# The sequence transform's A11 B11 for two blocks at once, in seven quarter products

## The chip, the core and the metric

The kernel runs on one core of one Trainium2 chip. The core has TensorE (matmuls from SBUF into PSUM), VectorE and ScalarE (elementwise work on SBUF and PSUM), GpSimd (here it only issues DMAs and a few memsets) and SyncE (it only issues DMAs). Each engine carries out its own instructions in the order in which the program gives them; semaphores tie the engines together. The metric is the device time of one execution in microseconds, the median of several runs. 0.2% is about what a measurement of this kernel can tell from no change.

## The reference

With S = 2048 rows, D = 512 columns and F = 1376 hidden units, all in f32:

```python
a = x @ dft_hid_re.T;  b = x @ dft_hid_im.T
y = dft_seq_re @ a - dft_seq_im @ b            # FNet mixing, real part
h = silu(x @ w1) * (x @ w3);  z = h @ w2       # SwiGLU
g = sigmoid((x * gate_w).sum(-1))
out = g * y + (1 - g) * z
```

The DFT matrices are inputs like any other.

## The kernel before, in words

**Precision.** Each f32 operand is split into a high part (rounded to the fp32r type by ScalarE, `high`, line 110) and a low part (source minus high, by VectorE, `low`, line 113). A product is then three matmuls: high x high, high x low, low x high (`mm3`, line 124 issues each). Nearly all the work of ScalarE and VectorE is in making these parts and the sums below. Two such parts of a 128x1024 operand are one `zo` buffer (`parts`), of which there are two in the first stage and four later; whole 128x1024 f32 operands lie in the `F4` buffers (`wide`). Both are handed out and given back in order, by lists that the program keeps while it is built.

**Seven products for eight.** Each big product is cut into 2x2 blocks and made by the Winograd form of Strassen's method: seven block products instead of eight, with sums of blocks ahead (T1 to T4 on the moving side, S1 to S4 on the stationary one) and sums of products behind. In the code a product has a name P1 to P7 and a form: P1 takes B11, P5 T1, P6 T2, P3 B22, P7 T3, P2 B21, P4 T4. P1 = A11 B11 is a part of all four results.

**Stage one, gate/up.** 22 steps; step n is one chunk of 128 hidden units against one half of the sequence, made by `gate_up(n)`. A step is 42 matmuls in seven products into PSUM banks X, Y and Z. What matters here is the order: the products that `gate_up` issues are X(4), Z(5), the first product of step n+3, X(3), Z(2), the second of step n+3, and X(6). Between them VectorE has, in this order: what `early` holds for the step (the low part of one operand of the second half, `xo`, and its sum, line 206), four sums for the weights of the next step (lines 245 to 248), `u4 += x` (line 368), the low part of these weights (`wb`), `u2 += z` (373), `u2 *= s1` (374), the low part of another weight (`wa`), and `g1 *= u4` (390), and last what `at_end` holds for the step. The X bank is read by line 368 and then accumulated into by X(6). The lists `early`, `ahead`, `second`, `mid`, `at_end` are dictionaries from a step to functions, filled by `do`. In the same stage the weights' wb parts go to DRAM and come back for the second half, the results h go to DRAM (line 323), and from step 9 on the operands of the next stages (w2 and the transformed inputs A1) are prepared, at the steps in `W2_AT` and `A1_AT`.

**Stage two, the sequence transform ("F").** Four blocks of 512 output columns. The stationary side is A = the transformed inputs (A1, A2, from x), the moving side are the DFT matrices (`cc`), whose blocks are loaded, summed, split and used once. `STEPS` is one list of steps (block, quarter of the contraction, product, form); an F block has 28 steps of 12 matmuls, four for each product. (b, n) below is step n of block b, counting blocks from 0. `advance(m)`, called in step m behind its matmuls, asks for the loads of step m+8 where F4 has a free buffer, makes the sum of step m+4 and the split of step m+3. A zo buffer comes free when TensorE has finished the step that used it. SyncE issues the loads in that order too, and waits in its queue for a buffer's last reader. When P1 is done, ScalarE copies its two banks into the banks of P2 (line 945), so that both go on accumulating. Results are multiplied by the gate and put to DRAM by `spill` (lines 815 to 818). Beside that, "late" pieces (one of w2, four of the hidden DFT `dd`) are loaded, summed, split and put to DRAM, by `late_load` and the functions after it, at given (b, n).

**Stages three and four** ("H", two blocks: h times w2; "Y", two blocks: the hidden DFT) use the same list of steps.

Of the kernel before, what the change touches and what calls it, by code (L numbers as in the profile page):

```python
# [7 lines left out]
F32 = mybir.dt.float32  # L8
# [4 lines left out]
P = 128  # L13
# [12 lines left out]
LOOK = 3  # L26
K = 9
TAIL = 256
W2_AT = (9, 11, 13, 15)
A1_AT = (12, 14, 16, 17, 18, 19, 20)  # L30


# [1 line left out]
def fnet_swiglu_gate_kernel(  # L34
# [103 lines left out]
    wbsp = dram.tile([NC, P, 2, 4, 256], F32, tag="wbsp", name="wbsp")  # L138
    zsp = dram.tile([4 * NTB * P, 1024], F32, tag="zsp", name="zsp")

    hsp = dram.tile([2, 4, (NP2 + 1) // 2, P, 1024], F32, tag="hsp", name="hsp")
    hlsp = dram.tile([2, P, 1024], F32, tag="hlsp", name="hlsp")

# [380 lines left out]
    for n, k in ((7, "B12"), (7, "B11"), (8, "B21"), (9, "B22")):  # L524
        do(early, n, lambda k=k: free(ST[1, k]))

    W2R = {}

    def load_w2(p):
# [67 lines left out]
    for k in range(LOOK + 2):  # L597
# [22 lines left out]
    STEPS = [(blk, q, k, form) for blk, nq in enumerate(NQ) for k, form in ORDER[blk]  # L620
             for q in range(nq)]
    START = [sum(NQ[:blk]) * len(CHAIN) for blk in range(NB + 1)]

    NEED = [(("B11", 0, 0), ("B12", 1, 1), ("B22", 2, 1), ("B21", 5 - (b == 0), 0))
            for b in range(NB - 1)]
# [10 lines left out]
    LOADS = sorted((START[blk] + n * nq - e * (blk > 0 or n != 1) + q, blk, k, q)  # L636
                   for blk, nq in enumerate(NQ) for q in range(nq) for k, n, e in NEED[blk])

    def z_rows(tb, k):
        return zsp[(tb * 4 + k) * P : (tb * 4 + k + 1) * P, :]  # L640

    def block(blk, k, q):
        if KIND[blk] == "F":
            return cc[blk, ("B11", "B12", "B22", "B21").index(k), q]
        if KIND[blk] == "H":
            return hsp[blk - NTB, ("B11", "B12", "B21", "B22").index(k), q]
        return z_rows(2 * (blk - NTB - 2) + (k in ("B12", "B22")), 2 * (k in ("B21", "B22")) + q)

    def cols(blk, q, form):

        return 512 if KIND[blk] == "H" and q == NQ[blk] - 1 else 1024

    def done(m, j):
        blk, q, k, form = STEPS[m]
        b = DONE[j].get(form)
        if b:
            free(RAW.pop((blk, b, q)))

    def sum_c(m):


        if not 0 <= m < len(STEPS):
            return
        blk, q, k, form = STEPS[m]
        b = {"T1": "B11", "T2": "B22", "T4": "B21"}.get(form)
        if b:
            n = cols(blk, q, b)
            t = RAW[blk, PLACE[form], q][:, :n]
            nc.vector.tensor_add(t, t, RAW[blk, b, q][:, :n])  # L669
        elif form == "T3":  # L670
            n = cols(blk, q, form)
            t = RAW[blk, "B11", q][:, :n]
            nc.vector.tensor_sub(t, RAW[blk, "B12", q][:, :n], t)  # L673
        done(m, 0)

    def split_c(m, parts_of=(0, 1)):
        if not 0 <= m < len(STEPS):
            return
        blk, q, k, form = STEPS[m]
        src = RAW[blk, PLACE.get(form, form), q]  # L680
# [33 lines left out]
    F4[:0] = [(f4_b, f"f4_{k}") for k in range(5 + LOOK, 13)]  # L714
    ZO[:0] = [(zo_b, f"zo_{k}") for k in range(2, 4)]
    def load_a2(p):

# [86 lines left out]
    XB, ZB, YB = ((4, 5), (6, 7)), (0, 2), (3, 1)  # L804
    U = {}

    def spill(blk, k, t, ps=None):


# [34 lines left out]
    def load_gate(blk):  # L844
        v = gsp if KIND[blk] == "F" else ngsp
        tbs = [blk] if KIND[blk] == "F" else [2 * (blk - NTB), 2 * (blk - NTB) + 1]
        GT[blk] = []
        for tb in tbs:
            t = ut.tile([P, 512], F32, tag="gate", name=f"gate{blk}_{tb}", bufs=2)
            nc.sync.dma_start(t, v[tb // 2, :, tb % 2 * 512 : (tb % 2 + 1) * 512])  # L850
            GT[blk].append(t)

    def load_nb(blk, k):
        tb = 2 * (blk - NTB - 2) + k // 2
# [17 lines left out]

    def step(m):
        blk, q, k, form = STEPS[m]
        kind = KIND[blk]
        if k == "P6" and kind != "Y" and q == 2 * (blk == 0):
            load_gate(blk)
        seeded = blk < NB - 1
# [111 lines left out]

            put(2, result)
        elif k == "P2" and seeded:
            put(1, lambda: spill(blk, 0, res("s1"), ps))
        elif k == "P2":
            plus("s1")
            spill(blk, 0, U["s1"])
        else:
            spill(blk, 1, res("c21"), ps)

    todo = {}  # L1000
    WL, HL = {}, {}
# [53 lines left out]
        free(*(HL.pop((blk, t)) for t in range(3)))  # L1055

    def at(blk, n, f, *a):
        todo.setdefault(START[blk] + n, []).append((f, a))

    at(1, 1, load_score, 1)  # L1060
    for p in range(NG):
# [7 lines left out]
    for g, n in enumerate((5, 3)):  # L1069
        for i in range(4):  # L1070
            at(g, n + i, gates, g, i)
    late = [(w2, w2sp, p) for p in range(len(W2_AT), NP2)] + [(dd, dsp, p) for p in range(KD)]
    for i, (src, sp, p) in enumerate(late):
        blk, b = 1 + i // 3, i % 3
        n = (10, 17, 24)[b]
        at(blk, n - (6, 5, 6)[b], late_load, i, src[p], ("u3", "s1", "u2")[b])
        at(blk, n, late_sums, i)
        at(blk, n + 1, late_split1, i)
        at(blk, n + 2, late_split2, i)
# [101 lines left out]
```

## Time and profile before

| | us |
|---|---|
| median of 3 runs | 674.63 (674.20 to 674.96) |
| the profiled execution | 674.75 |
| its span, first to last instruction | 673.0 |
| TensorE busy | 667.3 (99%) |
| VectorE busy | 577.2 (86%) |
| ScalarE busy | 370.0 (55%) |
| moved by DMA | 171 MB, mean 254 GB/s |

A row of the profile has the line, the engine, the operation, the names of output and inputs, their shapes and a count; then the busy time and the mean of one; then the idle time ahead of it and who ended that. Rows of the timeline begin with start and duration in us. In names, x2 and the like is a count of like instructions in one row; PE is TensorE, PEld its weight loads, DVE VectorE, ACT ScalarE, POOL GpSimd and SPq the DMA queue of SyncE. A matmul's duration is a latency and overlaps that of the next one.

### The profile page before, as it was taken

How to read it: one execution, taken by the hardware profiler on the slowest of the kernel's cores; microseconds unless marked ns; L12 is line 12 of the kernel's file. 1: busy time of each engine (PE TensorE's matmuls, PEld its weight loads, DVE VectorE, ACT ScalarE, POOL GpSimd, SP SyncE). 2: the span in 40 equal slices, each digit the busy share in tenths (PEclk: the TensorE clock that was granted, in tenths of full speed). 3: DMA queues.
4: the chain of work that ended last, by engine and by line, in shares of the span. 5: the costliest groups of instructions: out<-in, count | busy, mean ns of one | idle time of the engine just before them, and what ended most of it. 6: DMA issues, size and time to landing. Idle time of an engine off the chain costs nothing.

```text
span 673.0 us, 8613 instructions
## 1 busy us (share of the span) xinstructions
PE 667.3 (99%) x3101; PEld 580.5 (86%) x3101; DVE 577.2 (86%) x685; ACT 370.0 (55%) x472; POOL 61.9 (9%) x114
## 2 busy tenths in 40 slices
PE   8999999999999999999999999999999999999997
PEld 6888888888888888888888888888888888888886
DVE  6979877787679999988999799868798698798896
ACT  6765556656546874465454655444446446446452
POOL 0011112121110000101120101000000010010000
PEclk9999999999999999999999999999999999999999
DMA  7685655599986956644697277719888795784942
GB/s 296 213 304 222 236 217 205 205 349 372 424 364 240 361 196 236 250 155 152 239 373 298 80 254 276 281 34 349 308 323 238 238 378 166 312 300 173 339 126 94
DMA packets 46010, 171.23 MB, mean 254 GB/s; under 512 B 5520, under 2 KB 5904, under 8 KB 42256
## 3 DMA queue, kind: packets, MB, share of 16 engines
q1 hardware_dynamic: 33376, 118.90, 49.5%
q0 software_dynamic: 12160, 51.13, 19.3%
q10 hardware_dynamic: 432, 0.66, 0.3%
q8 instruction: 24, 0.39, 0.2%
q14 instruction: 18, 0.15, 0.1%
HBM read 115.34 MB, written 55.32 MB: 254 GB/s over the span
## 4 chain that ended last, share of the span: by engine, by line
PE 99%; DMA 1%; ACT 0%; SPq 0%; issue 0%
PE P L124 68%; PE X L124 16%; PE Z L124 8%; PE Y L124 4%; PE C L124 2%; DMA xs_B<-xt 1%; PE V L124 0%; PE P4left L124 0%; ACT xo L110 0%; ACT zc L834 0%; SPq L223 0%
## 5 line engine op out<-in xcount | busy, mean ns | idle before, releaser
L124 PE MATMUL P<-zo,a 128*128 128x512 f32 x1344 | 290.3, 379 | 0.0
L110 ACT ACTIVATE zo<-B 128x1024 fp32r<-128x1024 f32 (+1 forms) x182 | 185.5, 1022 | 182.8 <-PE P L124 99.6
L124 PEld LDWEIGHTS P<-zo,a 128*128 128x128 f32 x1344 | 253.9, 189 | 36.2
L113 DVE TENSOR_TENSOR zo<-B,zo 128x1024 fp32r<-128x1024 f32 (+1 forms) x182 | 213.5, 1178 | 33.1 <-ACT zo L110 32.4
L669 DVE TENSOR_TENSOR B<-B,B 128x1024 f32<-128x1024 f32 (+1 forms) x78 | 91.6, 1175 | 0.1
L124 PE MATMUL P<-zo,H 128*128 128x512 f32 x420 | 91.3, 379 | 0.0
L124 PEld LDWEIGHTS P<-zo,H 128*128 128x128 f32 x420 | 79.2, 189 | 11.8 <-issue 0.7
L124 PE MATMUL X<-xo,wb 128*128 128x512 f32 x378 | 88.9, 380 | 0.0
L124 PEld LDWEIGHTS X<-xo,wb 128*128 128x128 f32 x378 | 71.2, 189 | 10.6 <-DMA wb<-wbsp 0.3
L124 PE MATMUL P<-zo,Y 128*128 128x512 f32 (+1 forms) x336 | 71.6, 375 | 0.0
L124 PEld LDWEIGHTS P<-zo,Y 128*128 128x128 f32 x336 | 62.7, 189 | 8.7
L323 POOL DMA_DIRECT2D hsp<-h x40 | 21.9, 547 | 112.4 <-DVE h L374 67.9
L385 ACT ACTIVATE h<-X 128x512 f32<-128x512 f32 x21 | 12.5, 596 | 35.1 <-PE X L124 35.1
L124 PE MATMUL Z<-xo,wa 128*128 128x512 f32 x126 | 30.6, 379 | 0.0
L124 PE MATMUL Z<-xo,wb 128*128 128x512 f32 x126 | 30.6, 379 | 0.0
L673 DVE TENSOR_TENSOR B<-B,B 128x1024 f32<-128x1024 f32 (+1 forms) x26 | 30.6, 1177 | 0.0
L124 PE MATMUL X<-xo,wa 128*128 128x512 f32 x126 | 30.5, 379 | 0.0
L124 PE MATMUL Y<-xo,wa 128*128 128x512 f32 x126 | 30.5, 379 | 0.0
L124 PEld LDWEIGHTS X<-xo,wa 128*128 128x128 f32 x126 | 23.8, 189 | 3.4
L124 PEld LDWEIGHTS Y<-xo,wa 128*128 128x128 f32 x126 | 23.8, 189 | 3.4
L124 PEld LDWEIGHTS Z<-xo,wb 128*128 128x128 f32 x126 | 23.8, 189 | 3.4
L124 PEld LDWEIGHTS Z<-xo,wa 128*128 128x128 f32 x126 | 23.8, 189 | 3.4
(158 smaller groups left out, 548.6 us busy)
## 6 DMA issues: line engine op xcount, KB each, us to landing
B<-cc SPq DMA_DIRECT2D x64, 512.0 KB, 6.3
hsp<-h POOLq DMA_DIRECT2D x40, 256.0 KB, 4.3
wbsp<-wb POOLq DMA_DIRECT2D x8, 1024.0 KB, 4.2
wb<-wbsp SPq DMA_DIRECT2D x8, 1024.0 KB, 8.3
B<-hsp SPq DMA_DIRECT2D x16, 512.0 KB, 8.2
B<-zsp SPq DMA_DIRECT2D x16, 512.0 KB, 7.1
ws<-w SPq DMA_DIRECT2D x11, 512.0 KB, 5.4
H<-w2sp SPq DMA_DIRECT2D x5, 1024.0 KB, 8.5
```

The lines of the kernel that those rows point to most:

```text
L110: nc.scalar.activation(hi, src, AF.Copy)
L113: nc.vector.tensor_sub(lo, src, hi.bitcast(F32))
L124: nc.tensor.matmul(ps.rearrange("p (n a) -> p n a", a=2), u, turns(v)[:, some], **kw)
L323: nc.gpsimd.dma_start(hsp[g, b + k, j // 2, :, j % 2 * 512 : (j % 2 + 1) * 512], h)
L385: nc.scalar.activation(g1, x, AF.Silu)
L669: nc.vector.tensor_add(t, t, RAW[blk, b, q][:, :n])
L673: nc.vector.tensor_sub(t, RAW[blk, "B12", q][:, :n], t)
```

## The change

A11 B11 of block 2 and A11 B11 of block 3 have the same stationary side. The change takes B11 of both blocks as one matrix, cuts A11 (256 rows by 1024) and that matrix into 2x2 quarters, and makes the four quarters of the product by the same seven-product form one level down: m1 to m7, each of two steps of six matmuls.

- The eight P1 steps of blocks 2 and 3 go (`todo_p1`); what hung on them moves to the step after (`NEW`).
- The 14 new steps stand among steps (1,22) to (1,27) and (2,4) to (2,9), after the step that `AMONG` names: m1a; m1b and m6a; m6b; m7a; m7b; m4a and m4b; m2a; m2b; m5a; m5b; m3a; m3b.
- The sums of the moving quarters (T1 to T4 of the second level, each in two halves h) are made in gate/up: `load_quarters(h)` loads four 512 KB quarters into the two zo buffers at the end of step 2 (h = 0) and 5 (h = 1), `sum_quarter` makes one sum by VectorE and GpSimd puts it to DRAM (`tsp`), at the ends of steps 3, 4, 4, 5 and 6, 7, 8, 9. In the F stage they are loaded again like any other operand.
- The sums of the stationary side (`load_s`, `sums_s`, `high_s`, `low_s`) are made in block 1.
- `step_quarter` makes a step: m1 into bank 5, which ScalarE copies to bank 4; m6, m7 and m4 accumulate into bank 5, with ScalarE putting aside the state after m6 and after m7; m2 goes to bank 4; m5 to bank 7, to which VectorE adds the two states set aside (into banks 6 and 7); m3 into bank 6. Banks 4, 5 are then P1 of block 2, and 6, 7 of block 3. `seeds` makes the copies for P2.
- Of the late pieces, those at (1,17), (1,24) and (2,17) go to (3,10), (3,17) and (5,4). The first w2 piece of gate/up goes from step 9 to 10. F4 gets one buffer more; the gates one less, and for H a different one; block 1's P2 and P4 results leave from another buffer (u3).

```diff
-W2_AT = (9, 11, 13, 15)
+W2_AT = (10, 11, 13, 15)
...
+    def load_quarter(h, b, t):
+        BQ[h, b] = t
+        nc.sync.dma_start(t, cc[2 + (b[2] == "2"), 0, 2 * (b[1] == "2") + h])
+
+    def load_quarters(h):
+        for b in ("b11", "b12"), ("b21", "b22"):
+            t = BQ[h, b] = parts(f"q{h}{b[0]}")
+            v = t.bitcast(F32).rearrange("p h a n -> p h (a n)")
+            for i in range(2):
+                load_quarter(h, b[i], v[:, i])
+
+    def sum_quarter(h, i):
+        to, u, v = (("b11", "b12", "b11"), ("b22", "b22", "b11"),
+                    ("b12", "b22", "b12"), ("b21", "b21", "b22"))[i - 1]
+        nc.vector.tensor_sub(BQ[h, to], BQ[h, u], BQ[h, v])
+        nc.gpsimd.dma_start(tsp[i - 1, h], BQ[h, to])
+
+    for h, at_n in enumerate(((2, 3, 4, 4, 5), (5, 6, 7, 8, 9))):
+        do(at_end, at_n[0], load_quarters, h)
+        for n, i in zip(at_n[1:], (1, 3, 2, 4)):
+            do(at_end, n, sum_quarter, h, i)
+        do(at_end, at_n[4], lambda h=h: free(BQ[h, ("b11", "b12")], BQ[h, ("b21", "b22")]))
...
+    AMONG = {(1, 22): ("m1a",), (1, 23): ("m1b", "m6a"), (1, 24): ("m6b",), (1, 25): ("m7a",), (1, 26): ("m7b",),
+             (1, 27): ("m4a", "m4b"), (2, 4): ("m2a",), (2, 5): ("m2b",), (2, 6): ("m5a",),
+             (2, 7): ("m5b",), (2, 8): ("m3a",), (2, 9): ("m3b",)}
...
+            if blk in (2, 3) and k == "P1":
+                todo_p1.append(START[blk] + n)
+                continue
...
+    def step_quarter(m):
+        _, h, k, _ = STEPS[m]
+        zt = ZT.pop(m)
+        z = zt.rearrange("p h a n -> p h (a n)")
+        to = {"m2": 4, "m5": 7, "m3": 6}.get(k, 5)
+        own = k in ("m1", "m5")
+        if own and h == 0:
+            MB[to] = bank(to, f"quarter{to}")
+        for i in range(2):
+            b = slice(i * 512, (i + 1) * 512)
+            mm3(MB[to], *quarter(k, h, i), z[:, 0, b], z[:, 1, b], own and h == i == 0, h == i == 1,
+                not own)
+        free(zt)
+        advance(m)
+        if h == 0:
+            return
+        if k == "m1":
+            MB[4] = bank(4, "quarter4")
+            nc.scalar.activation(MB[4], MB[5], AF.Copy)
+        elif k == "m6":
+            MB["u"] = ut.tile([P, 2, 512], F32, tag="u2", name="uu")
+            nc.scalar.activation(MB["u"][:, 0], MB[5], AF.Copy)
+        elif k == "m7":
+            nc.scalar.activation(MB["u"][:, 1], MB[5], AF.Copy)
+            free(*SF[0])
+        elif k == "m2":
+            seeds(2, MB[4], MB[5])
+        elif k == "m5":
+            MB[6] = bank(6, "quarter6")
+            nc.vector.tensor_add(MB[6], MB[7], MB["u"][:, 0])
+            nc.vector.tensor_add(MB[7], MB[7], MB["u"][:, 1])
...
+    LATES = (1, 10, "u3"), (2, 10, "u3"), (3, 10, "u3"), (3, 17, "s1"), (NTB + 1, 4, "s1")
```

More of the change, by code (lines that the diff above doesn't have):

```diff
@@ L649, in cols @@
     def cols(blk, q, form):
-        return 512 if KIND[blk] == "H" and q == NQ[blk] - 1 else 1024
+        return 512 if form[0] != "m" and KIND[blk] == "H" and q == NQ[blk] - 1 else 1024
     def done(m, j):
         blk, q, k, form = STEPS[m]
+        if k[0] == "m":
+            return free(RAW.pop((4, k, q))) if j and form != "B11" else None
         b = DONE[j].get(form)
@@ new lines, in high_s, with low_s, quarter @@
+    def high_s(i):
+        SF[i] = [take(F4, [P, 1024], F32R, f"s{i}{k}") for k in "hl"[: 2 - i]]
+        if i:
+            SF[i].append(ut.tile([P, 1024], F32R, tag="s1", name="s1l"))
+        high(SF[i][0], flat(SR[i]))
+    def low_s(i):
+        low(*SF[i], flat(SR[i]))
+    def quarter(k, h, i):
+        kk = 2 * h + i
+        if len(QUARTERS[k]) == 3:
+            _, r, half = QUARTERS[k]
+            w = A1[4 * half + kk][:, :, 1, r * P : (r + 1) * P]
+            return w[:, 0], w[:, 1]
+        t, at = {"m6": (0, 0), "m7": (0, P), "m3": (1, 0), "m5": (1, P)}[k]
+        return [v.rearrange("p (k n) -> p k n", k=4)[:, kk, at : at + P] for v in SF[t]]
```

89 lines of the change are left out of this document (73 added, 16 removed).

## The prediction

> **What bounds the kernel now.** I read the page's totals and its chain first, then the busy time step by step, then the order of instructions in the steps that the change touches.
>
> ```profile
> span 673.0 us, 8613 instructions
> PE 667.3 (99%) x3101; PEld 580.5 (86%) x3101; DVE 577.2 (86%) x685; ACT 370.0 (55%) x472; POOL 61.9 (9%) x114
> PE 99%; DMA 1%; ACT 0%; SPq 0%; issue 0%
> L124 PE MATMUL P<-zo,a 128*128 128x512 f32 x1344 | 290.3, 379 | 0.0
> ```
>
> TensorE is busy 99% of the span and the chain that ends last is TensorE almost alone, so a matmul less is time less and a pause of TensorE is time more. The group of the sequence transform gives the price of one: 290.3 / 1344 = 0.216 us (379 ns is its latency, which overlaps the next one). VectorE has 86%, and that is a mean. The same for gate/up steps 4 to 8, which are 42 matmuls or 9.07 us each:
>
> ```profile
> 51.51:60.57 9.06, 9.06 (x44) 7.93 (x43) 8.13 (x13) 5.60 (x8) 1.55 (x3) 1.00 0.57 217
> 60.57:69.64 9.07, 9.07 (x44) 7.94 (x43) 8.43 (x13) 5.60 (x8) 1.63 (x3) 1.00 0.62 231
> 69.64:78.71 9.07, 9.07 (x44) 7.94 (x43) 8.42 (x12) 4.87 (x7) 1.62 (x3) 1.00 0.45 175
> 78.71:87.77 9.06, 9.06 (x44) 7.93 (x43) 7.74 (x12) 5.60 (x8) 1.63 (x3) 1.00 0.90 333
> 87.77:96.84 9.07, 9.07 (x44) 7.94 (x43) 7.10 (x11) 4.77 (x7) 1.16 (x3) 1.00 0.58 217
> ```
>
> (stretch, length, then busy time of TensorE, weight load, VectorE, ScalarE, GpSimd, then granted clock, DMA share, GB/s.) VectorE is free for 0.9, 0.6, 0.6, 1.3 and 2.0 us in these five steps, and one, two, one, one and one subtractions are put there.
>
> **What it removes.** A11 B11 of two blocks is 2 x 4 steps of 12 matmuls, 96. Seven quarter products of 2 steps of 6 are 84. Twelve go: 12 x 0.216 = **-2.59 us**.
>
> **What it adds in gate/up.** Eight `sum_quarter` subtractions of 128x1024, queued at the ends of steps 3, 4, 4, 5, 6, 7, 8, 9. What is behind them on VectorE:
>
> ```profile
> 56.95 0.69 DVE L368 TENSOR_TENSOR u<-u,X 128x512 f32<-128x512 f32 x1 [0.19 <-PE X L124]
> 59.27 2.75 PE L124 MATMUL X<-xo,wb 128*128 128x512 f32 x12
> 61.40 0.69 DVE L390 TENSOR_TENSOR h<-h,u 128x512 f32<-128x512 f32 x1
> 63.26 1.23 DVE L206 TENSOR_TENSOR xs_B<-xs_B,xs_B 128x1024 f32<-128x1024 f32 x1
> 64.40 0.42 DVE L245 TENSOR_TENSOR wu<-ws 128x256 f32<-128x256 f32 x1
> 65.53 0.42 DVE L248 TENSOR_TENSOR wu<-ws,wu 128x256 f32<-128x256 f32 x1
> 65.98 1.06 ACT L110 ACTIVATE wb<-wu 128x1024 fp32r<-128x1024 f32 x1 [0.69 <-DVE wu L248]
> 66.02 0.69 DVE L368 TENSOR_TENSOR u<-u,X 128x512 f32<-128x512 f32 x1
> 67.08 1.23 DVE L113 TENSOR_TENSOR wb<-wu,wb 128x1024 fp32r<-128x1024 f32 x1 [0.38 <-ACT wb L110]
> 68.34 2.75 PE L124 MATMUL X<-xo,wb 128*128 128x512 f32 x12
> 70.46 0.69 DVE L390 TENSOR_TENSOR h<-h,u 128x512 f32<-128x512 f32 x1
> 75.08 0.69 DVE L368 TENSOR_TENSOR u<-u,X 128x512 f32<-128x512 f32 x1 [0.19 <-PE X L124]
> 77.40 2.75 PE L124 MATMUL X<-xo,wb 128*128 128x512 f32 x12
> 79.53 0.69 DVE L390 TENSOR_TENSOR h<-h,u 128x512 f32<-128x512 f32 x1 [0.96 <-ACT h L385]
> 84.15 0.69 DVE L368 TENSOR_TENSOR u<-u,X 128x512 f32<-128x512 f32 x1 [0.19 <-PE X L124]
> 93.21 0.69 DVE L368 TENSOR_TENSOR u<-u,X 128x512 f32<-128x512 f32 x1 [1.32 <-PE X L124]
> ```
>
> This is VectorE's order in a step: L390 closes the step before, then (new) the sums, then the split and sum of xo, four sums of wu, and L368, which reads bank X. The step's last product, at the head of the x12 rows (59.27, 68.34, 77.40), accumulates into that bank, so TensorE may not start it before L368 has read. L368 ends at 57.64, 66.71 and 75.77, some 1.63 us early. A delay above that stops TensorE. Step 5 has no idle time at all but the 0.38 us in which wb waits for ScalarE, and that wait moves along with wu.
>
> One more subtraction is taken at the pitch of its nearest likeness: L206 at 63.26, next start at 64.40, 1.14 us; the other bound is its whole 1.22 us. [...]
>
> For the lag from VectorE to TensorE:
>
> ```profile
> 5.80 1.29 DVE L113 TENSOR_TENSOR xo<-xs_B,xo 128x512 fp32r<-128x512 f32 x2 [0.15 <-ACT xo L110]
> 7.15 0.19 PEld L124 LDWEIGHTS C<-xo,wa 128*128 128x128 f32 x1 [0.29 <-DVE xo L113]
> ```
>
> 7.15 - 7.09 = 0.06 us. Now step by step, times as in the trace of before:
> - Step 4, one sum: L368 is late by 1.14 - 0.19 = 0.95, within 1.63. No stop. L390 at 61.40 comes 1.0 later (of the 1.14, about 0.15 goes into small gaps).
> - Step 5, two sums: 1.0 + 2.28 = 3.28 late, ends 69.99; product due at 68.34, starts 70.05: TensorE stops **1.71**. L390 at 70.46 is 3.27 late.
> - Step 6, one: ends 75.77 + 3.27 + 1.14 - 0.19 = 79.99; due 77.40: 2.65 in all, so 0.94 more. L390 at 79.53 absorbs its 0.96 of idle and is 3.45 late.
> - Step 7, one: ends 84.84 + 3.45 + 1.14 - 0.19 = 89.24; due one step (9.07) after 77.40, at 86.47: 2.83 in all.
> - Step 8, one: it has no xo sum, and L368 has 1.32 idle before it. L390 of step 7 is 4.4 late (3.45 + 1.14 - 0.19), so L368 ends 93.90 - 1.32 + 4.4 + 1.14 = 98.1, due 95.54: 2.6, less than TensorE is late already. Nothing more; after it VectorE gains on TensorE.
>
> Stops in gate/up: **+2.83 us**. Bounds: 0, if the lateness stays below 1.63, and 3.3 at 1.22 a sum. I take 2.83, as every operand has a row. The W2 work moved from step 9 to 10 leaves room for the last two sums, in steps that are looser (step 8 is free for 2.0 us): nothing. Without that room L368 would be late by one sum, within 1.63.
>
> **What it adds around blocks two and three.** `m6a` follows `m1b` directly on TensorE, and both use bank 5: ScalarE must copy m1 to bank 4 in between.
>
> ```profile
> 61.86 1.46 PE L124 MATMUL Z<-xo,wb 128*128 128x512 f32 x6
> 63.16 1.46 PE L124 MATMUL X<-xo,wa 128*128 128x512 f32 x6
> 63.36 0.60 ACT L359 ACTIVATE u<-Z 128x512 f32<-128x512 f32 x1 [0.70 <-PE Z L124]
> 362.76 0.58 ACT L945 ACTIVATE P<-P 128x512 f32<-128x512 f32 x1 [0.32 <-PE P L124]
> ```
>
> The next group could start at 63.16, the copy starts at 63.36: 0.20 + 0.58 + 0.06 = **+0.84 us**. Bounds 0.6 (the copy alone) and 1.9 (a 1.06 us split ahead of it on ScalarE). The copies of m6 and m7 have a block-one step behind them and are hidden.
>
> VectorE there: quarter steps last 1.30 us and bring a split, at the 1.14 pitch, so they leave almost nothing, where the eight old steps left 1.45 each.
>
> ```profile
> 344.43 1.28 DVE L815 TENSOR_TENSOR zs<-P,gate 128x512 f32<-128x512 f32 x2
> 349.67:360.04 10.37, 10.37 (x50) 9.08 (x49) 10.37 (x11) 5.89 (x6) 2.17 (x4) 1.00 1.02 393
> ```
>
> From step (1,22) to m3b TensorE has 12 x 2.59 + 14 x 1.30 = 49.3 us. VectorE has 26 splits and 10 sums at 1.14, two results of 1.28 (first row), the two additions of m5 at the same price and a split of S: 46.0 us. The sums and first split of S, ahead of that, and six more splits on ScalarE (55% busy) go where two of the late pieces leave block one: nothing, or without that room some 4 x 0.69 us of VectorE in a full stretch. So it fits, with little to spare; in the second row VectorE is full today without stopping TensorE. Two places can still stop it. m3a waits for m5's first addition, which may stand behind one split: 0 to 1.1 us. And loads come later: ten of 512 KB are added here (m3 to m7), buffers run out, and by the order in which they come free the fourth B22 load of block two goes last, behind m3a's split, some 1.5 us after step (2,7).
>
> ```profile
> B<-cc SPq DMA_DIRECT2D x64, 512.0 KB, 6.3
> dsp<-late_0h POOLq DMA_DIRECT2D x4, 512.0 KB, 4.8
> ws<-w SPq DMA_DIRECT2D x11, 512.0 KB, 5.4
> DMA to landing us min/median/max: 3.0/4.0/5.1
> ```
>
> (KB each, us from issue to landing; the last row is of the B loads between 372 and 400 us, where the queues are quiet.) With 6.3 it lands at 7.8; its sum and the split behind that are done at 10.1, where step (2,10) is due after m5b, (2,8), m3a, (2,9), m3b, at 9.1: 1.0 late; with 4.0, in time. I take **+0.5** for both places together; bounds 0 and 2.1.
>
> The eight loads and eight stores of 512 KB in gate/up fall into 45 to 90% DMA share (steps 4 to 8 above) and are asked for ten or more us ahead: hidden, but for the queue that they stop, below.
>
> Sum: -2.59 + 2.83 + 0.84 + 0.5 = +1.6 on the profiled execution's 674.75, which stands 0.12 above the median of 674.63; so **676.2 us**.
>
> **Rivals.**
> *The sums hide (faster).* Place: L368 of step 5. If its lateness stays under 1.63 us there, and so behind it, the subtractions are free. For it: each single sum stays under that; only two at one step end pass it. Against: no idle row is there to take the second. Then -2.59 + 0.84 + 0.5, or 673.4, and 672.9 without the last term.
> *Half of it.* VectorE recovers about half of the 2.83 in gaps that I count as fixed: 674.8, no change that can be told.
> *The DMA queue of SyncE stops (slower still).* The second half's b21 load goes where the first half's T4 is stored from. T4 ends at 73.7 + 0.6 + 1.2 = 75.5, lands 4.8 later, 80.3; until then SyncE holds the ws load of step 7, the second of the row below, which goes out by 66.35 today.
>
> ```profile
> 56.82 9.53 SPq L223 DMA_DIRECT2D ws<-w  x2
> 85.90 0.83 ACT L110 ACTIVATE wa<-ws 128x768 fp32r<-128x768 f32 x1
> ```
>
> It would land at about 80.3 + 1.0 (three issues of 0.33) + 2.7 (1 MB ahead of it at the 393 GB/s of the row above) + 5.4 = 89.4; its split is due near 90.3 (85.90 today, 4.4 late). From about 0.9 us more, ScalarE stops, and what TensorE waits for behind it; twice the landing would stop it for 4: some 2.5 us, 678.7.
> *The clock drops.* Rows at the start, before the clock is granted, have TensorE at 3.90 us for 11 matmuls of 512, 0.355 each; a stretch like that in place of 0.216 costs 1.5 us, 677.7 in all. Against: stops here are at most 1.7 us and the clock was 1.00 in all stretches above.
>
> ```profile
> 0.78 3.90 PE L404 MATMUL wps<-const-bfloat16-1.0 128*128 128x512 bf16 x11 [0.78 <-PEq L1170]
> ```
>
> [...]
>
> **How the numbers follow.** Forecast (675.0 to 677.5) 0.50, sums hidden 0.22, half 0.13, queue 0.11, clock 0.04. This kernel's measurements tell 0.2% (1.35 us) from no change, so faster is below 673.3 and slower above 676.0. Faster: the hidden case and little else, 0.23. Slower: 0.37 of the forecast's 0.50, queue and clock, 0.52. Same 0.25. Range 672.4 (hidden, no last term, a little off) to 678.9 (queue).
>
> **What would show it.** The first stop of TensorE at the end of step 5, on L368, 1 to 2 us, shorter ones in steps 6 and 7, none later in gate/up; one stop of 0.8 between m1 and m6 on ScalarE; the sequence transform's matmuls 12 fewer. It is wrong if TensorE runs through steps 4 to 8, or if the largest stop waits on a DMA.

## The result, and the profile after

The changed kernel takes 681.52 us (median of 5, 679.96 to 681.84) against 674.63 (674.20 to 675.14): ratio 1.0097, interval 1.0083 to 1.0112. It is 6.9 us slower; 676.2 was predicted, and the time lies above the range. Its profiled execution took 679.96 and is the lowest of the five. The ledger below is for that one; what the other runs have more comes with the last experiments.

The page of the kernel after, in the order in which the prediction showed that of before:

```profile
span 677.8 us, 8698 instructions
PE 667.7 (99%) x3089; PEld 577.2 (85%) x3089; DVE 598.3 (88%) x707; ACT 378.0 (56%) x483; POOL 66.2 (10%) x122
PE 84%; DVE 8%; DMA 4%; issue 2%; ACT 1%; SPq 0%; DVEq 0%; ACTq 0%; POOLq 0%
```

The twelve matmuls are gone (3089 in place of 3101). TensorE's share is 99% as before, but the chain that ends last is no longer TensorE alone: VectorE has 8% of it and DMA 4%. Where they came in shows in TensorE's timeline. The rows are the x12 groups at the head of which X(6) stands, for steps 3 to 6 and 11 to 13, with the two other stops between and behind them; a stop is the figure in brackets:

```profile
50.45 2.75 PE L124 MATMUL X<-xo,wb 128*128 128x512 f32 x12
60.71 2.88 PE L124 MATMUL X<-xo,wb 128*128 128x512 f32 x12 [1.03 <-DVE u L369]
72.11 2.88 PE L124 MATMUL X<-xo,wb 128*128 128x512 f32 x12 [2.04 <-DVE u L369]
82.13 2.88 PE L124 MATMUL X<-xo,wb 128*128 128x512 f32 x12 [0.66 <-DVE u L369]
...
127.67 2.75 PE L124 MATMUL X<-xo,wb 128*128 128x512 f32 x12
132.15 1.56 PE L124 MATMUL X<-xo,wa 128*128 128x512 f32 x6 [0.44 <-ACT sc L310]
138.69 2.88 PE L124 MATMUL X<-xo,wb 128*128 128x512 f32 x12 [0.97 <-DVE u L369]
147.88 2.75 PE L124 MATMUL X<-xo,wb 128*128 128x512 f32 x12
...
352.05 0.70 PE L124 MATMUL quarter<-zo,s0h 128*128 128x512 f32 x2 [0.67 <-ACT quarter L934]
```

Line 369 here is line 368 of before. A bracket leaves out the latency of the matmuls ahead of the stop, so the full price is read from the starts: a step without a stop lasts 9.06 us (122.73 to 131.79 of the next fence). Against before, the starts become late by 1.20 more in step 4, 2.33 in step 5, 0.95 in step 6 and 0.2 in steps 7 and 8, together 4.7; between 127.67 and 147.88 by 2.1, of which 0.25 is won back by the end of the stage. Gate/up starts 0.24 later, so the F stage starts 6.8 later (213.93 against 207.15). F itself lasts 1.65 less: the 2.59 of the matmuls, less 0.83 at the m1 copy (its full price by the starts) and 0.1. H and Y last as long as in before. That is +5.1 at the last row of TensorE; the span is 4.8 longer, and the profiled execution 5.2.

The same rows of before, for comparison:

```profile
122.73 2.75 PE L124 MATMUL X<-xo,wb 128*128 128x512 f32 x12
131.79 2.75 PE L124 MATMUL X<-xo,wb 128*128 128x512 f32 x12
140.86 2.84 PE L124 MATMUL X<-xo,wb 128*128 128x512 f32 x12
```

So three things stand beside the forecast: a stop already in step 4, where none was expected; a longer one in step 5; and two stops around step 11, where nothing was expected.

**Step 4.** VectorE, ScalarE and SyncE's queue of the kernel after, in order of time, and behind them the two rows of before that answer to 52.74 and 54.50:

```profile
31.25 2.16 SPq L532 DMA_DIRECT2D q0b<-cc  x4
37.44 23.01 SPq L224 DMA_DIRECT2D ws<-w  x3
52.74 0.84 ACT L110 ACTIVATE wa<-ws 128x768 fp32r<-128x768 f32 x1 [3.43 <-DMA ws<-w]
53.62 0.96 DVE L113 TENSOR_TENSOR wa<-ws,wa 128x768 fp32r<-128x768 f32 x1 [2.34 <-ACT wa L110]
54.50 0.68 DVE L391 TENSOR_TENSOR h<-h,u 128x512 f32<-128x512 f32 x1
```

```profile
49.11 0.84 ACT L110 ACTIVATE wa<-ws 128x768 fp32r<-128x768 f32 x1
52.33 0.69 DVE L390 TENSOR_TENSOR h<-h,u 128x512 f32<-128x512 f32 x1 [0.43 <-ACT h L385]
```

The four quarter loads, queued at the end of step 2, go out from 31.25 on, one behind the other. The weight load (`ws`) of step 3 is asked for at 37.44, behind them in SyncE's queue, and its split on ScalarE starts at 52.74, after a wait of 3.43 for the DMA: the load took 15.2 us to land, against 6.2 for the same load in before. L391 starts 1.93 later than L390 in before, if the start's 0.24 is taken off. Only then comes the first sum (55.10). VectorE thus enters step 4 already later than the 1.63 us that it has to spare. Once TensorE has stood for VectorE there, nothing of the 1.63 is left for step 5, and its two sums are paid in full: 2.33, against 2 x 1.14.

The DMA in the stretches around it, three of before and then the second and third of after (stretch, length, busy times of the five engines, clock, DMA share, GB/s):

```profile
31.20:37.40 6.20, 6.20 (x30) 5.43 (x29) 5.42 (x9) 3.57 (x6) 1.63 (x3) 1.00 0.98 340
37.40:46.40 9.00, 9.00 (x44) 7.87 (x43) 7.08 (x11) 5.61 (x8) 1.63 (x3) 1.00 0.92 364
46.40:55.00 8.60, 8.60 (x42) 7.53 (x41) 6.81 (x9) 5.61 (x8) 1.62 (x3) 1.00 0.60 231
```

```profile
37.40:46.40 9.00, 9.00 (x44) 7.87 (x43) 6.85 (x12) 5.61 (x8) 1.63 (x3) 1.00 1.02 406
46.40:55.00 8.60, 8.60 (x42) 7.47 (x41) 4.90 (x8) 4.74 (x7) 1.08 (x2) 1.00 1.02 419
```

Before, the first stretch is already at 98% and the second at 92%: the quarter loads were put where the DMA had no room, and 2 MB of them pushed what came behind. In the kernel after both stretches are full (1.02).

**Step 11.** The kernel after, the two w2 pieces of steps 10 and 11:

```profile
123.72 0.54 POOL L582 DMA_DIRECT2D w2sp<-w2a  x1 [1.35 <-ACT u L360]
129.12 0.42 ACT L110 ACTIVATE w2a<-w2r 128x256 fp32r<-128x256 f32 x1 [4.50 <-DMA w2sp<-w2a]
130.18 0.83 ACT L110 ACTIVATE wa<-ws 128x768 fp32r<-128x768 f32 x1
131.04 0.96 DVE L113 TENSOR_TENSOR wa<-ws,wa 128x768 fp32r<-128x768 f32 x1 [3.05 <-ACT wa L110]
```

The same operation as at 129.12 in before:

```profile
119.60 0.41 ACT L110 ACTIVATE w2a<-w2r 128x256 fp32r<-128x256 f32 x1
```

Each w2 piece takes both zo buffers of the first stage. With the pieces in steps 10 and 11 the second must wait until the first has been stored: the store goes out at 123.72 and lands 5.3 us later, and `high` of the second piece (129.12) has stood for it on ScalarE. Queued behind it are the high part of `wa` and the copy `sc`, which frees bank X for TensorE's next product, and on VectorE everything behind the low part of `wa`. In before one step lay between the two pieces: the store had gone out at 109.7, ten us ahead of 119.60, and no such wait is there.

### The profile page after: what moved, and what is told of

Read it like the earlier page. It is cut to its first block, busy times and chain, and to the rows that moved or that the text cites. A ratio compares the mean times of both kernels' runs of the same rounds, so it can differ in the third digit from the quotient of the medians.

```text
span 677.8 us, 8698 instructions
## 1 busy us (share of the span) xinstructions
PE 667.7 (99%) x3089; PEld 577.2 (85%) x3089; DVE 598.3 (88%) x707; ACT 378.0 (56%) x483; POOL 66.2 (10%) x122
## 4 chain that ended last, share of the span: by engine, by line
PE 84%; DVE 8%; DMA 4%; issue 2%; ACT 1%; SPq 0%; DVEq 0%; ACTq 0%; POOLq 0%
PE P L124 55%; PE quarter L124 12%; PE X L124 10%; PE Z L124 5%; DMA ws<-w 2%; PE Y L124 2%; DVE wa L113 1%; DVE xo L113 1%; DMA xs_B<-xt 1%; DVE xs_B L207 1%; DMA w2sp<-w2a 1%; DVE q0b L546 1%; DVE wu L247 1%; DVE wu L249 0%; DVE h L391 0%
## 5 line engine op out<-in xcount | busy, mean ns | idle before, releaser
L110 ACT ACTIVATE zo<-B 128x1024 fp32r<-128x1024 f32 x178 | 180.8, 1021 | 165.7 <-DVE B L730 65.3
L113 DVE TENSOR_TENSOR zo<-B,zo 128x1024 fp32r<-128x1024 f32 x178 | 208.3, 1178 | 22.6 <-ACT zo L110 21.6
L124 PE MATMUL P<-zo,a 128*128 128x512 f32 x960 | 209.7, 379 | 0.0
L124 PEld LDWEIGHTS P<-zo,a 128*128 128x128 f32 x960 | 181.4, 189 | 25.9
L124 PE MATMUL quarter<-zo,a 128*128 128x512 f32 x324 | 72.0, 379 | 0.0
L124 PEld LDWEIGHTS quarter<-zo,a 128*128 128x128 f32 x324 | 61.2, 189 | 8.7
L113 DVE TENSOR_TENSOR wa<-ws,wa 128x768 fp32r<-128x768 f32 (+1 forms) x22 | 19.3, 880 | 9.1 <-ACT wa L110 9.1
```

Of the source, the lines that this page charges most:

```text
L110: nc.scalar.activation(hi, src, AF.Copy)
L113: nc.vector.tensor_sub(lo, src, hi.bitcast(F32))
L124: nc.tensor.matmul(ps.rearrange("p (n a) -> p n a", a=2), u, turns(v)[:, some], **kw)
```

## The experiments

**The w2 pieces alone.** The kernel before with one edit:

```diff
-W2_AT = (9, 11, 13, 15)
+W2_AT = (10, 11, 13, 15)
```

> The kernel before with one edit: the first piece of w2 goes from gate/up step 9 to 10, so that two pieces follow each other in steps 10 and 11. Theory (the moved piece makes ScalarE wait for the store of the piece ahead from the same zo buffer): ScalarE waits 4 to 5 us on the w2a store in step 11, TensorE stops by 1.5 to 2.5 us around steps 11 and 12, time 676.1 to 677.1. Rival (the prediction's: the moved piece costs nothing by itself, the stop there comes from the added DMA and sums): 674.6 within 0.5.

Measured: 677.16 (676.61 to 679.20) against 674.39, ratio 1.0041 (1.0025 to 1.0058). TensorE's only stops in it are these:

```profile
127.23 1.56 PE L124 MATMUL X<-xo,wa 128*128 128x512 f32 x6 [0.85 <-ACT sc L309]
133.77 2.88 PE L124 MATMUL X<-xo,wb 128*128 128x512 f32 x12 [0.97 <-DVE u L368]
```

The pair of the kernel after, without anything else of the change; the theory holds (the median is 0.06 above its range) and its rival (no cost) is out. A term that the prediction set to nothing costs 2 to 3 us alone: 2.4 at X(6) of step 12 in this profile, 2.8 between the medians.

**The sums left out.** The kernel after without the eight subtractions; the quarters are stored as loaded, so the T1 to T4 products are made of other data.

```diff
-        nc.vector.tensor_sub(BQ[h, to], BQ[h, u], BQ[h, v])
```

> The changed kernel without the eight subtractions of the quarters in gate/up (the loaded quarters are put to DRAM as they are, so the output is not the reference's); loads, stores and all else stay. Theory (VectorE's added work stops TensorE on the line that reads X, a late ws load adds to it): the stops of steps 4 to 7, 4.7 us in the trace, fall to under 0.5, time about 677. Rival one (the late ws load of step 3 alone is the cause, the sums hide): stops stay near 4.7, time 681.5. Rival two (the sums are half of it): 679.2.

Measured: 676.25 (674.99 to 681.27), ratio 1.0036 (1.0017 to 1.0054). Its ScalarE at the late split of step 3, and its timeline of TensorE around the two places:

```profile
51.87 0.84 ACT L110 ACTIVATE wa<-ws 128x768 fp32r<-128x768 f32 x1 [2.68 <-PE X L124]
...
68.46 2.75 PE L124 MATMUL X<-xo,wb 128*128 128x512 f32 x12
...
122.85 2.75 PE L124 MATMUL X<-xo,wb 128*128 128x512 f32 x12
134.00 2.88 PE L124 MATMUL X<-xo,wb 128*128 128x512 f32 x12 [0.97 <-DVE u L369]
```

In step 5 and in step 11 (68.46, 122.85) X(6) stands 0.12 behind before (68.34 and 122.73 there): the stops of steps 4 to 7 are all gone, with the loads and stores in place. Those around step 11 are there, 2.1 us. The `ws` load is late here too (the split of step 3 is 2.6 behind before at 51.87, VectorE then 1.2), but 1.2 is within the 1.63. So in this execution the quarter loads cost nothing on their own; it is the sums, or sums and loads together, that stop TensorE. Both rivals of the expectation are out.

**The loads behind the weight load.** The kernel after, with the second pair of the first half's quarters loaded one step later, so that two of the four loads stand behind the `ws` load of step 3:

```diff
-        do(at_end, at_n[0], load_quarters, h)
+        for j, b in enumerate((("b11", "b12"), ("b21", "b22"))):
+            do(at_end, at_n[0] + (j if h == 0 else 0), load_quarters, h, (b,))
```

> The changed kernel with the loads of b21 and b22 of the first half at the end of step 3 in place of step 2, so behind the ws load that came 15 us late. Theory: that load lands in time, the weight split of step 3 is no longer late, the stops of steps 4 to 7 fall from 4.7 to the 2.8 us that the prediction worked out for the sums alone, time 679.6. Rival (the late load is hidden under the sums' own lateness): 681.5, stops unchanged.

Measured: 678.50 (677.94 to 679.79), ratio 1.0058 (1.0043 to 1.0073). Its TensorE timeline, and the `wa` split of step 3:

```profile
48.89 0.84 ACT L110 ACTIVATE wa<-ws 128x768 fp32r<-128x768 f32 x1
...
59.05 2.75 PE L124 MATMUL X<-xo,wb 128*128 128x512 f32 x12
69.72 2.88 PE L124 MATMUL X<-xo,wb 128*128 128x512 f32 x12 [1.45 <-DVE u L369]
79.74 2.88 PE L124 MATMUL X<-xo,wb 128*128 128x512 f32 x12 [0.66 <-DVE u L369]
```

The split waits for no DMA, step 4 has no stop, and the starts of steps 5, 6 and 7 to 8 are late by 1.61, 0.95 and 0.21 more. That is 2.77; the prediction had 1.71, 0.94 and 0.18. This kernel is the one that was predicted, but for the w2 pieces, and its time is 1.1 below the expectation. The order of the loads is worth 4.7 - 2.8 = 1.9 us in the profiles and 3.0 between the medians; the median of the kernel after lies 1.6 above its profiled execution, of which more below.

**The w2 pieces further apart.** The kernel after with:

```diff
-W2_AT = (10, 11, 13, 15)
+W2_AT = (10, 12, 14, 16)
```

> The changed kernel with the four w2 pieces at steps 10, 12, 14, 16 in place of 10, 11, 13, 15, so that none follows another directly. Theory (a store of the piece ahead holds the zo buffer): the 2.0 us of stops near steps 11 and 12 go, time 679.5. Rival (the pieces then meet the preparation of A1 in steps 12, 14 and 16 and VectorE is over its step there): stops move and the time stays 681.5 or rises.

Measured: 686.30 (685.88 to 687.00), ratio 1.0172 (1.0155 to 1.0189). The stops around step 11 are gone and one of 5.0 us stands in their place, seven steps later:

```profile
179.35 7.05 DMA w2sp<-w2a
...
186.94 8.99 DMA xr<-xn
...
195.95 0.42 DVE L172 TENSOR_TENSOR xr<-xr 128x256 f32<-128x256 f32 x1 [8.28 <-DMA xr<-xn]
...
197.95 4.54 PE L124 MATMUL X<-xo,wb 128*128 128x512 f32 x12 [5.00 <-DVE u L369]
```

The first two rows are of the chain that ends at the stop. The fourth w2 piece, now in step 16, is stored from the zo buffers at 179.35, which takes 7.05 us; a `wb` load (line 231) that takes such a buffer stands in SyncE's queue until 186.8, the load of an A1 piece stands behind it, and VectorE stands 8.28 us for that. The rival was right that the stop would move, but not in its reason: VectorE is not over its step, it waits, and the cause is once more a store that holds a zo buffer. The twelve matmuls behind the stop take 4.54 us where they took 2.88 behind shorter ones. That is the clock: the stretch from 197.9 to 202.5 of this profile has a granted clock of 0.63.

**m6 one step after m1.**

```diff
-    AMONG = {(1, 22): ("m1a",), (1, 23): ("m1b", "m6a"), (1, 24): ("m6b",), (1, 25): ("m7a",), (1, 26): ("m7b",),
+    AMONG = {(1, 22): ("m1a",), (1, 23): ("m1b",), (1, 24): ("m6a", "m6b"), (1, 25): ("m7a",), (1, 26): ("m7b",),
```

> The changed kernel with m6a one step later, behind step (1,24) and directly ahead of m6b, so that a whole block-one step lies between m1 and m6 on bank 5. Theory: the 0.67 us stop on ScalarE's copy goes, nothing else moves, 0.7 to 0.9 us less than the changed kernel, 680.7. Rival (the short steps then starve TensorE of splits): the stop goes elsewhere, 681.5 or more.

Measured: 680.65 (679.53 to 680.83), ratio 1.0078 (1.0058 to 1.0099). The stop of 0.67 is gone; one of 0.22, on the addition behind m5, is new, and the F stage lasts 0.48 less. The median is 0.9 below that of the kernel after, but that is not this edit's price alone: in this profile the `ws` load landed after 14.4 us in place of 15.2, the stop in step 4 is 0.21 in place of 1.03 (that in step 5 is 2.05), and H has two new stops, which the last experiments explain.

**The sums on GpSimd.**

```diff
-        nc.vector.tensor_sub(BQ[h, to], BQ[h, u], BQ[h, v])
+        nc.gpsimd.tensor_sub(BQ[h, to], BQ[h, u], BQ[h, v])
```

> The changed kernel with the eight subtractions on GpSimd in place of VectorE. Theory (what counts is VectorE's queue): the stops of steps 4 to 7 fall under 0.5 as without the subtractions, the others stay, 676 to 677. [...]

Measured: 687.52 (686.98 to 689.04), ratio 1.0181 (1.0157 to 1.0204). VectorE and GpSimd in step 4:

```profile
55.10 2.38 POOL L546 TENSOR_TENSOR q0b<-q0b 128x1024 f32<-128x1024 f32 x1
55.12 3.46 DVE L207 TENSOR_TENSOR xs_B<-xs_B,xs_B 128x1024 f32<-128x1024 f32 x1
```

L207 takes 1.23 us in before (L206 there). Here it starts 0.02 us behind a GpSimd sum and lasts 2.2 us longer, nearly the sum's whole length. At 69.55 it is L246: 2.62 us in place of 0.42, behind a sum of 2.36. So a sum moved to GpSimd cost VectorE 2.2 us at these two places, in place of 1.14. What makes the later one longer no run shows.

A mix of four edits (the split loads; the sums on GpSimd, done by step 8; the w2 piece back in step 9; m6 one step later), of which the cut shows three places, keeps that cost:

```diff
-W2_AT = (10, 11, 13, 15)
+W2_AT = (9, 11, 13, 15)
...
-        nc.vector.tensor_sub(BQ[h, to], BQ[h, u], BQ[h, v])
+        nc.gpsimd.tensor_sub(BQ[h, to], BQ[h, u], BQ[h, v])
...
-    for h, at_n in enumerate(((2, 3, 4, 4, 5), (5, 6, 7, 8, 9))):
+    for h, at_n in enumerate(((2, 3, 4, 4, 5), (5, 6, 7, 7, 8))):
```

> All three stops taken away at once: sums on GpSimd and done one step sooner, w2 pieces back at steps 9, 11, 13, 15, b21 and b22 of the first half loaded behind the ws load, m6a one step later. Theory (the stops of steps 4 to 7, of the w2 pair and of m1 are the whole loss): 12 matmuls less and no stop, 674.4 - 2.6 = 671.8, up to 672.8 with small rests. Rival (something else of the change costs time, as the 1.5 us by which its plain runs lie above its profiled one, or GpSimd's sums do): 674 or more.

Measured: 685.70 (683.52 to 686.49), ratio 1.0151 (1.0125 to 1.0177). The stops around step 11 and at m6 are gone; the sums stop TensorE by 0.23, 3.90, 0.84 and 3.11.

**The high parts of the second w2 piece later.** The split-loads kernel, with `high` of that piece at the head of step 12 and not in step 11, behind the high part of `wa` on ScalarE:

```diff
-            do(mid, n, high_w2, p)
+            if p == 1:
+                do(early, n + 1, high_w2, p)
+            else:
+                do(mid, n, high_w2, p)
```

> The kernel with the split loads of the first half, and with the high parts of the second w2 piece made at the start of step 12 in place of the middle of step 11, so that the store of the first piece (5 us to landing) is over before its buffer is written. Theory: ScalarE's wait on that store and the two stops behind it (2.0 us) go, the stops of steps 5 to 7 (2.8 us) stay: 676.5. Rival (the wait only moves to step 12): 678.5.

Measured: 677.65 (677.13 to 678.88), ratio 1.0049 (1.0035 to 1.0062). This lies between theory and rival, 0.85 below the split loads alone. The first of the two stops is gone, the second, at X(6) of step 12, stays at 0.97: there VectorE itself waits 1.34 for the high parts. In before L368 of that step ends at 131.59, and X(6) starts at 131.79, so only 0.2 us is to spare.

**All these causes lessened at once.** Every pair of quarters is loaded ahead of, or well behind, the weight loads, no step end has two sums except step 8, and two of the edits above are in (m6 one step later, the high parts later); the diff is cut to the loads and sums:

```diff
+    do(at_end, 1, lambda: load_quarters(0, (("b11", "b12"),)))
...
-    for h, at_n in enumerate(((2, 3, 4, 4, 5), (5, 6, 7, 8, 9))):
+    for h, at_n in enumerate(((2, 3, 4, 6), (7, 8, 8, 9))):
+        for n, b in zip(((1, 2), (5, 7))[h], (("b11", "b12"), ("b21", "b22"))):
```

> The changed kernel with its eight sums on VectorE at the ends of steps 2, 3, 4, 6, 7, 8, 8, 9 in place of 3, 4, 4, 5, 6, 7, 8, 9, each pair of quarters loaded by itself where no ws load waits behind it, the w2 edit of the run beside it and m6a one step later. Worked out as in the prediction, VectorE's lateness at the X line is then 0, 0.6, 1.5, 1.3 and 1.5 us in steps 3 to 7, under the 1.63 that TensorE leaves: no stop in gate/up. Theory (sums, w2 pair, late load and m1 are all of the loss): 674.5 - 2.6 = 672, to 672.8 with small rests, faster than both kernels. Rival (a further cost of the change, as the added DMA traffic): 674 or more.

Measured: 675.27 (673.84 to 677.02, 11 runs) against 674.64, ratio 1.0011 (1.0002 to 1.0020): 6 us better than the kernel after, but 2.5 to 3.3 above the expectation: the rival, a further cost, was right. In its profile TensorE stops 0.19 in step 5, 0.97 in step 12, 0.22 behind m5, and, new, 0.33 and 0.47 in the H stage. Ahead of these last two VectorE waits:

```profile
559.92 0.43 DVE L154 TENSOR_TENSOR c21p<-s1p 128x256 f32<-128x256 f32 x1 [1.83 <-DMA nbsp<-zc]
```

The late piece that the change put at (5,4) makes its sums in the buffer from which block 4's result (`zc`) is still being stored. In the profile of the kernel after VectorE did not wait there. H lasts 88.75 us from the start of its first row to that of its last one in that profile (502.37 to 591.12; the 99.0 of the next expectations counts to the end of that row, and is the same H) and 90.1 here (497.19 to 587.29). Of the nine profiles with the piece at (5,4) four have this wait at 1.46 to 2.06 us, and H is 0.9 to 1.6 longer in them (here, without the sums, with m6 later, with the high parts later); one has 0.48 of it, and four have none.

**The late piece elsewhere.** First at the end of block 3, on the kernel after, and on the spread version (there with `high` of the second w2 piece in step 11 again, but behind the low part of `wa`):

```diff
-    LATES = (1, 10, "u3"), (2, 10, "u3"), (3, 10, "u3"), (3, 17, "s1"), (NTB + 1, 4, "s1")
+    LATES = (1, 10, "u3"), (2, 10, "u3"), (3, 10, "u3"), (3, 17, "s1"), (3, 24, "u2")
```

> The changed kernel with one late piece moved: the last of LATES goes from (5,4) to (3,24), with buffer u2. Theory: at (5,4) its sums wait for the buffer from which block 4's first result is still being stored, in most executions by 1.0 to 1.5 us, and the plain runs of the changed kernel (681.5) lie above its profiled one (680.0) for that; so this kernel's runs come to 680.0 to 680.4, and its H stage lasts 99.0 us. Rival, the 1.5 us between the profiled and the plain runs have nothing to do with the late piece: 681.5 as before. Second rival: at (3,24) the piece falls on the end of block 3, whose results leave from the buffers that it needs; then VectorE or SyncE is late there and the time is 682 or more.

> The version with the sums spread (respread) and two edits: the last late piece at (3,24) with buffer u2, and the high parts of the second w2 piece queued on ScalarE between the two x products behind the low part of wa, in step 11, in place of the head of step 12. Theory: the three stops that were left there (0.97 in step 12, 0.33 and 0.47 in H, the last of which stands in every version of the change) go but for the 0.2 in step 4: 673.6 in its profile less 1.0 to 1.8, so 672.0 to 673.0, faster than before. Rival: the high parts in step 11 delay ScalarE's silu and with it VectorE's closing product of the step, and the stop only moves: 674 to 675.3, no change from before.

Measured: 685.37 (684.89 to 686.52), ratio 1.0160 (1.0144 to 1.0175), and 679.24 (677.32 to 680.67), ratio 1.0062 (1.0045 to 1.0079). Each is 4 us slower than the same kernel with (5,4); the second fits neither the theory nor the rival of its expectation. In the first, TensorE's stop in step 5 and its first one in H, and the granted clock (behind the five busy times) in a stretch behind the former:

```profile
72.49 4.54 PE L124 MATMUL X<-xo,wb 128*128 128x512 f32 x12 [2.04 <-DVE u L369]
...
521.23 0.48 PE L124 MATMUL P<-zo,H 128*128 128x512 f32 x1 [1.70 <-ACT zo L110]
```

```profile
73.28:76.68 3.40, 3.40 (x10) 2.67 (x9) 3.37 (x5) 2.52 (x4) 1.08 (x2) 0.50 0.71 289
```

The second rival was right: the piece's parts take F4 buffers when the operands of H need them (a load for H stands in SyncE's queue until 507.4 for a store of the piece that left at 499.55), and H is 5.5 us longer in this profile. And step 5 shows something that the profile of the kernel after does not. The stop is the same, 2.04 to the last digit, but here the clock falls: it is 0.50 for 3.4 us, so TensorE loses 1.7 us, and the twelve matmuls take 4.54 in place of 2.88. The kernel after just behind the same stop:

```profile
72.00:76.70 4.70, 4.59 (x21) 3.95 (x22) 4.14 (x7) 3.80 (x7) 1.08 (x2) 1.00 0.78 297
```

So a stop of 2 us can cost the clock or not: five profiles have this one at 2.04 or 2.05, and in one of them the clock fell. Why equal stops end differently no run shows.

What a fall costs the kernel depends on what stands behind it. In the profile with (3,24) the stop of step 6 is gone, since TensorE, being slower, now arrives there late itself: from X(6) of step 5 to that of step 8 TensorE falls back by 1.79 against before, where the kernel after falls back by 1.17, so the fall costs 0.6. In the profile with the w2 pieces further apart nothing of the kind follows, and TensorE falls back by 1.79 in the step behind the stop.

Every run gives its mean granted clock, and a loss of 1.7 in 680 is 0.0025: the kernel after has 0.997 in two of its five runs (681.21 and 681.84), 1.00 or 0.999 in the others. The kernel with m6 later, which has the same 2.05 in step 5, has 0.997 in three of four, and one of these is its fastest run; the one with (3,24) alone has 0.997 or 0.998 in three of four. The kernel with the loads split and that with the high parts later, whose longest stop is 1.45, the one with the w2 edit alone and the two spread versions with a late piece at (5,4) or (5,6) are at 0.999 or 1.00 in all 34 of their runs; the three kernels with stops of 3.9 and 5.0 are at 0.99 to 0.998 in all 12 of theirs. Not every case is that plain: the kernel without the sums and the spread one with (3,24), whose stops are below 1.2 in their profiles, have 0.997 once in ten and twice in six; what stopped TensorE in those executions is not recorded.

Then two steps later, again on both kernels:

```diff
-    LATES = (1, 10, "u3"), (2, 10, "u3"), (3, 10, "u3"), (3, 17, "s1"), (NTB + 1, 4, "s1")
+    LATES = (1, 10, "u3"), (2, 10, "u3"), (3, 10, "u3"), (3, 17, "s1"), (NTB + 1, 6, "s1")
```

> The changed kernel with its last late piece at (5,6) in place of (5,4), same buffer. Theory: at (5,4) its sums wait in many executions for block 4's result store, which still reads the buffer; two steps (5.2 us) later that store has landed. The plain runs (681.5) then come down to what the changed kernel's profiled execution shows, 680.0 to 680.5, and H lasts 99.0 us. Rival: the plain runs lie above the profiled one for another reason, a DMA whose landing varies in gate/up: 681.2 to 681.8 as before. Second rival: the piece's splits, now at (5,7) and (5,8), meet the loads of hl at (5,7) to (5,9), which need the same buffers, and the time rises above 682.

> The version with the sums spread (respread), the last late piece at (5,6), and the high parts of the second w2 piece behind the low part of wa in step 11. Theory: the stops of 0.97 in step 12 (0.70 with this order) and the 1.3 us in H go; 675.3 less 1.3 less 0.3 is 673.7, with a range from 673.2 to 674.2, a little faster than before (674.5). Rival, the spread of respread's runs (673.8 to 677.0) has its cause in gate/up, where eight loads and eight stores of 512 KB are added to a DMA that is 50 to 90% busy: then the median stays at 674.8 to 675.4 and the spread stays too.

Measured: 680.61 (679.46 to 681.95), ratio 1.0091 (1.0077 to 1.0106), and 674.04 (673.63 to 674.60, 11 runs) against 674.56, ratio 0.9991 (0.9982 to 1.0000). The late piece's first sum in the latter:

```profile
560.06 0.42 DVE L154 TENSOR_TENSOR c21p<-s1p 128x256 f32<-128x256 f32 x1
```

VectorE does not wait, H lasts 88.8 (496.91 to 585.67), and the runs, which spread over 3.2 us with (5,4), lie within 1.0, as expected. (This version has `high` of the second w2 piece where the one with (3,24) has it.) On the kernel after the median falls by 0.9, between the theory and the rival, but the spread of 2.5 us stays, so five runs don't show that fall.

Why the median of the kernel after lies 1.6 us above its profiled execution is thus open in part. The traces of its relatives give three sizes: the wait in H, 0.9 to 1.6; the landing of step 3's `ws` load, which moves TensorE's lateness in step 4 from 0.4 (landing after 14.4 us, with m6 later) over 1.2 (15.2, the kernel after) to 1.9 (16.0, the first kernel here); and the clock, 0.6 behind the stop of step 5. Its clock of 0.997 alone does not sort the runs: 681.52 and 681.72 have 1.00 and 0.999. Which of the three each run had is not recorded.

The last version is the best one: 0.5 us below before, too little to tell from no change (the interval reaches 1.0000). TensorE's longest stop in gate/up there:

```profile
133.70 2.88 PE L124 MATMUL X<-xo,wb 128*128 128x512 f32 x12 [0.71 <-DVE u L369]
```

X(6) of step 12 still starts 1.9 later than in before (133.70 against 131.79). F lasts 2.1 less than in before, and gate/up takes 1.8 of that back even so.

## Why the prediction was wrong, step by step

- **What bounds the kernel, and the price of a matmul:** right. TensorE's stops add up to the loss, and the F stage is shorter by 1.65: the 2.59 less the copy (0.83) and 0.1.
- **The eight sums in gate/up, +2.83:** right in mechanism, place and size, where nothing else disturbs it: 2.77 with the loads split, the stops in steps 5, 6 and 7 as worked out. In the kernel after it is 4.7, since VectorE came in late; the sign named for it, the first stop in step 5, failed with that. The price per sum, 1.14, held for a single one: in the kernel after the next operation starts 1.14 behind the sum in step 4 (55.10 to 56.24) and in step 6 (76.52 to 77.66). The two of step 5 take 2.39 to the next start (65.12 to 67.51), 0.11 more than two such prices.
- **"The eight loads and eight stores of 512 KB in gate/up ... hidden, but for the queue that they stop":** wrong, 1.9 us in the profile. I looked at when these loads are needed and at the DMA share of steps 4 to 8. I did not look at the share where they go out (98% and 92%), nor at what stands behind them: a `ws` load that is used 12 us later in before and landed after 15.2 here. Without the sums a lateness of 1.2 was covered; with them it used up the room in which step 4's sum was to hide.
- **The queue that they stop** (the rival at 678.7): SyncE did stand in the second half's loads, 12.2 us from 70.06, but the `ws` load of step 7 came in time, and there is no stop on it. Right that it is hidden.
- **"The W2 work moved from step 9 to 10 ... nothing":** wrong, 2.1 us in the profile, and 2.8 alone between the medians. I priced the work that leaves step 9, and that the piece lands next to the one of step 11, which shares its two buffers, was not asked. The store's landing of 5.3 us (the stores of the first two pieces took 4.3 to 7.2 in before) became a wait.
- **The copy of m1, +0.84:** 0.67 by the bracket, 0.83 by the starts. Right.
- **VectorE and the late load around blocks two and three, +0.5:** about 0.1; the 0.22 behind m5 shows when m6 is moved. In its bounds, on the low side.
- **The late pieces that moved to (3,10), (3,17) and (5,4):** not priced at all. The last one waits for a result store and costs 0.9 to 1.6 us of H in some executions, though not in the profiled one of this kernel; (3,24) would have cost 4 more.
- **The clock** (the rival at 677.7, chance 0.04): TensorE's loss in a fall is 1.7 (a clock of 0.50 for 3.4 us), near the 1.5 worked out, in part by luck: the 0.355 is a mean over slow and fast matmuls (in before 0.43 from start to start at first, 0.22 from 3.64 us on; the first entry of the granted clock in that trace, 1.00, is at 3.55 us). Behind the stop of step 5 such a fall cost the kernel only 0.6 (the profile with (3,24)). Against the rival I held that stops are at most 1.7. Through the loads the one in step 5 became 2.0, and by the mean granted clock (0.997) there was a fall in two of five runs.

The forecast's sign held, and 5.3 us were missing. They are 1.9 (loads), 1.8 (w2 pieces, what is left of the 2.1 at the end of the stage), 0.4 (the start and small rests) and 1.6 that the median has over the profiled execution, whose cause is open in part, less 0.4 of the 0.5 for VectorE and the late load that did not come.

## What to carry to other kernels

Where TensorE is at 99%, a change that adds work elsewhere is priced by three questions for each transfer or piece that it adds or moves: how full the DMA is at the time of issue, what stands behind it in the same queue and when that is used, and which earlier piece holds its buffers until when. Room on an engine is spent once: here 1.9 us of lateness and 1.14 of a sum met in a step that had 1.63, and together they stopped the bound engine. A piece moved by one step cost 2.0 to 2.8 us, about what the twelve matmuls give. And a piece that is moved away from a collision can meet the same one elsewhere: a w2 store held ScalarE in step 11 and, with the pieces later, SyncE's queue ahead of step 18.

## What was not expected of the hardware

- After equal stops of 2.04 to 2.05 us the granted clock fell in one of five profiles: to 0.50, for 3.4 us. TensorE lost 1.7 us, the kernel 0.6, because the slower TensorE found the next stop already over. By the mean clock no fall was seen in eight runs with a longest stop of 1.45, and one in every run with 3.9 and more.
- A 512 KB load that landed 6.2 us after its issue in before took 15.2 behind four others of that size, with the DMA at 1.02 share and 406 to 419 GB/s for 17 us.
- A GpSimd subtraction of 128x1024 f32 took 2.36 to 2.39 us, about twice VectorE's 1.22, and two VectorE instructions (L207 and L246) that started 0.02 us behind one lasted 2.2 us longer: 3.46 in place of 1.23, and 2.62 in place of 0.42.
